# Sums of gathered rows and the next gathers behind a pair's fill while the first places are found

## The chip, the cores and the metric

The kernel runs on one core of a Trainium2 chip. A core has five engines, each with its own in-order queue of instructions: PE (matrix multiplication; results go to PSUM, a small memory of banks), DVE (vector work), ACT (activation functions and copies), POOL (here: places of rows, and the gathers), and SP (which issues DMA transfers). The profile lists PE's loading of weights as PEld. The metric is the device time of one execution in microseconds, as the median of several runs. The profile is of one further execution.

## What is computed

A layer norm of x (2048 tokens, 512 features) feeds two branches, and both are added to x. Branch A is attention with 32 heads of 16 features and one shared key and value. Branch B is a layer of 4096 small experts ("PEER"): for each token and each of 32 heads, scores against two sets of 64 keys give the best two of each, the best two of their four sums name two experts, and each expert adds a gated row.

```python
q1 = q[..., :dk]; q2 = q[..., dk:]
s1 = einsum("nhd,ed->nhe", q1, k1); s2 = einsum("nhd,ed->nhe", q2, k2)
i1 = argsort(-s1)[..., :2]; i2 = argsort(-s2)[..., :2]
cand = t1[..., :, None] + t2[..., None, :]          # four sums per head
top_s, top_e = best two of cand, and their experts
g = softmax(top_s)
act = gelu(einsum("nd,nhkd->nhk", xn, u[top_e]))
out = einsum("nhk,nhk,nhkd->nd", g, act, v[top_e])
return x + attention(xn) + out
```

## The kernel before

The 2048 tokens are 16 tiles of 128, in four blocks (phases) of 4 tiles. Experts are handled in two ways. For tokens of blocks 0 and 1 the rows of u and v are **gathered**: one indirect DMA on POOL (L1231) fetches, for 128 tokens, one expert's row of u and of v each (4 KB a token) into one of 12 buffers (`NGB`). There are 512 such gathers. For blocks 2 and 3 a dense form is used, with one-hot rows and matmuls against all experts.

**Places.** `score_thread` finds which experts each token takes. Its order `SEQ` is block 0 with chunks 0 to 7 (a chunk is four heads), block 1 with chunks 0 and 1, block 2 with 0 to 7, then the dense work of block 2, block 1 with 2 to 7, and block 3. While it does block 0 it also makes the weights of the next chunk (`wp_make`: matmuls pw L648, transposes pwt L661, ACT's scaled copy L663, squaring passes L619, and DVE's low half L664). One `item` is 12 matmuls psc (L720), 8 MAX8 (L733) and 4 FIND_INDEX8 (L740) on DVE. After four items `batch` makes the indices on POOL (L784 to L809) and puts four entries into the dictionary `IDX`. psc, pw and pwt share three PSUM tiles (tag x).

**The paired loop.** From the loop `for d in range(half + 24)` on, each step d handles a pair of key blocks of attention, by `att_steps`. The instructions are issued in the order in which the code runs, and each engine takes its own in that order:

1. two score tiles (PE sc L452, two PSUM tiles of tag s, and ACT's exponential L459),
2. the value products of the step before (PE pv L469),
3. `mid()`: on ACT the tanh of finished gathers (L1259), squaring passes over expert rows (L1379) and other waiting items; on DVE the dot products of gathered u rows (`dots`, L1243) and the weights of the sums (`weigh`, L1266, which needs the tanh); then the closure `go`,
4. two more score tiles and exponentials,
5. `fill()`: `run_scores` takes pieces of `score_thread` until a sum of assumed costs is reached, and then runs what stands in `POST_FILL`.

**The closure `go`** has four kinds of work: the sums of gathered v rows into the token's accumulator (`adds`, DVE L1278, two or three a step); the items of `CHAIN`, three small DVE instructions after every fourth dot (gq L1252, gy L1253, ga L1254; gy is the input of the tanh of the next step); the items of `rest`, such as the gates of a batch (L792, L814 to L816); and up to four new gathers, each into the buffer that a sum has just read. Now and then it also queues the store of a finished token tile. `go` runs at once inside `mid`, so ahead of items 4 and 5, but for the time in which one-hot rows are formed (`dense_on[0] == 2`): then it stands in `POST_FILL`, behind the fill.

A copy on POOL that the first step issues starts at 121.5 us (L1445). `IDX` is only added to: four entries for each batch of blocks 0 and 1, and none for blocks 2 and 3. `NC` is 8 and `TPH` is 4.

Of the kernel before, what the change touches and what calls it, by code (L numbers as in the profile page):

```python
# [33 lines left out]
NC = 8  # L34
TPH = GT
# [26 lines left out]
def tile_kernel(ctx, tc, exact, flag, x, wq, wkv, wo, wqT, kT, uv, ub, vb, out):  # L62
# [519 lines left out]
    def experts_out(t):  # L582
        acc, last = ACC[t], t // GT == QB[3]
        assert last or t in DONE_A
        store(lambda: nc.sync.dma_start(d_part[t] if last else out[t * P:(t + 1) * P, :], acc))
        LIVE.discard(t)
# [102 lines left out]
    def met_most():  # L689
        assert meets[0] == NPH * NC  # L690
        m = PK["met"] = small.tile([P, 1], F32, name="mm", bufs=1)
        nc.vector.reduce_max(m, most.rearrange("p t h k -> p (t h k)"), axis=AX.X)

    def met_flag():
        m = PK.pop("met")
        p = xtile("pm")
        nc.tensor.transpose(p[:1, :P], m, ident)
        r = small.tile([1, 1], F32, name="prd", bufs=1)
        nc.vector.reduce_max(r, p[:1, :P], axis=AX.X)
        nc.vector.tensor_scalar(flag, r, 0.0, None, op0=OP.is_ge)  # L700
# [44 lines left out]
    IDX, G = {}, {}  # L745
# [516 lines left out]
    def weigh(n):  # L1262
        if n not in WT and n < a_ready[0] // SB:
            ga, th = GA.pop(n), TH.pop(n)
            w = small.tile([P, SB], F32, name="w", bufs=3)
            nc.vector.scalar_tensor_tensor(w, th, 1.0, ga, op0=OP.add, op1=OP.mult)  # L1266
            WT[n] = w
# [17 lines left out]
    def gathers(most):  # L1285
        while g_next[0] < NSL and g_next[0] < a_next[0] + NGB - lent[0] and most > 0:
            gather(g_next[0])
            g_next[0] += 1
            most -= 1

    def dots(to):
        while d_next[0] < min(to, NSL):
            dot(d_next[0])
            d_next[0] += 1

    def adds(most):
        while a_next[0] < a_ready[0] and most > 0:
            add(a_next[0])
            a_next[0] += 1
            most -= 1  # L1300

    def tanhs(to):
        while a_ready[0] + SB <= to:
            tanh(a_ready[0] // SB)
            a_ready[0] += SB
# [8 lines left out]
    def run(fns):  # L1314
        todo = fns[:]
        fns.clear()
        for fn in todo:
            fn()
# [6 lines left out]
    def flush():  # L1325
        posts()
        for _ in range(2):
            for fns in (ON_ACT, PARTS, LAST, LATER, BEHIND):
                run(fns)
            ON_ACT.extend(LATER_ACT)  # L1330
            LATER_ACT.clear()
        run(ON_ACT)
        run(BEHIND)
# [65 lines left out]
    def norm_steps(d):  # L1399
        j, r = divmod(d - 24, 2)  # L1400
        if r == 0 and 0 <= j < NB // 2:
            NU[j] = norm_rows(j)
        j, r = divmod(d - 26, 2)
        if 0 <= j < NB // 2:
            on_act(lambda t=NU[j]: norm_sum(j, t, r))
        if d == 58:
            norm_most()
        if d == 60:
            norm_factors()

    dense_on, quiet = [0], [0]
# [3 lines left out]
    def run_scores(until=None, key=None):  # L1415
        while (until is not None and spent[0] < until) or (key is not None and key not in IDX):
            posts()
            try:
                cost = next(sgen)
            except StopIteration:  # L1420
                spent[0] = 1e9
                posts()
                return
            if cost is None:

                if key is None:
                    return
                continue
            spent[0] += cost

    STEPS = 512


    def att_steps(d, mid, fill):
        i = 2 * d
        run(STORES)
# [16 lines left out]
        if 0 < i <= STEPS:  # L1453
# [3 lines left out]
            if pk == 14:  # L1457
                unit_tail(pu)
        mid()
        if 0 < i < STEPS:  # L1460
            scores(u, kc + 1, 0)
# [40 lines left out]
    def score_steps(n):  # L1502
        for _ in range(n):
            spent[0] += next(sgen)
# [122 lines left out]
    with tc.manual_schedule(engines=ENGINES):  # L1627
        nc.vector.tensor_copy(PK["mm"][96:128], PK["mm"][:32])
        run(AFTER)
        score_steps(3)  # L1630
        done0 = spent[0] - 5.4
        half = STEPS // 2
        pos, since = 0.0, half
        for d in range(half + 24):


            if dense_on[0] != 0:
                since = d
            if dense_on[0] == 1:
                pos += 2.35 if d < half * 3 // 4 else max(0.0, NSL - pos) / max(half - 3 - d, 1)  # L1640
            else:
                pos += (2.6 if len(IDX) < NC * TPH else 2.45 if 0 <= d - since < 32 else 2.05, 0, 0.25, 1.5, 0.5)[dense_on[0]]

            todo = max(min(int(pos + 0.001), g_next[0]) - d_next[0], 0) if d else 0

            def mid():
                post = POST[:]
                POST.clear()
                for act, _ in post:
                    act()  # L1650
                tanhs(d_next[0])
                room = ROOM - 0.65 * len(ON_ACT) - 0.7 * len(LAST)
                run(ON_ACT)
                ON_ACT.extend(LATER_ACT)
                LATER_ACT.clear()
                run(LAST)
                while PARTS and (room > 0.7 or len(PARTS) > 3):
                    PARTS.pop(0)()
                    room -= 0.75
                LAST.extend(LATER)  # L1660
                LATER.clear()
                rest = BEHIND[:]
                BEHIND.clear()

                dots(d_next[0] + todo - 1)
                if a_ready[0] > a_next[0]:
                    weigh(a_next[0] // SB)
                dots(d_next[0] + 1 if todo > 0 else 0)
                for _, fn in post:
                    fn()  # L1670
                sums = min(a_ready[0] - a_next[0], max(todo, 3) if d < half else 4)
                if dense_on[0] > 2:
                    sums = min(sums, 2)
                if quiet[0] > 0:
                    quiet[0] -= 1
                    sums = 0
                if dense_on[0] == 2:
                    run(CHAIN)

                def go():  # L1680
                    n = sums
                    while rest or CHAIN or n > 0:
                        if n > 0:
                            adds(1)
                            n -= 1
                        elif not rest:
                            run(CHAIN)
                        if CHAIN:
                            CHAIN.pop(0)()
                        if rest:  # L1690
                            rest.pop(0)()
                    gathers(4)

                    for _ in range(1 if d < half - 4 else NT):
                        if OUTS:
                            experts_out(OUTS.pop(0))

                if dense_on[0] == 2:
                    POST_FILL.append(go)
                else:  # L1700
                    go()

            aim = done0 + (FILL - done0) * (d + 1) / half if d < half else 1e6

            def fill():
                run_scores(until=min(aim, spent[0] + MOST))
                run(POST_FILL)

            norm_steps(d)
            att_steps(d, mid, fill)  # L1710
            if d == half - 26 and not exact:
                met_most()
            if d == half - 16 and not exact:
                met_flag()
        flush()
        run(STORES)
        while a_next[0] < NSL:
            dots(NSL)
            run(CHAIN)
            tanhs(d_next[0])  # L1720
            adds(SB)
            run(STORES)
            gathers(NGB)
        assert not OUTS
        run(STORES)
# [42 lines left out]
```

## Time and profile before

| | |
|---|---|
| median of 3 runs | 1788.83 us (1785.12 to 1790.47) |
| the profiled execution | 1779.54 us, its span 1777.7 us |
| granted PE clock, mean | 0.991 |
| DMA, mean of the span | 265 GB/s |
| gathers (L1231) | 512, 1068 ns of POOL each |
| sums (L1278) | 512, 744 ns of DVE each |
| dots (L1243) | 512, 681 ns of DVE each |

How to read the rows. A row of the groups has line, engine, operation, tiles written and read, shapes and count, then busy us, mean ns of one, and the idle time of the engine just before them with what ended it. A row of the timeline has start, duration, engine, line, operation; in brackets stands the idle time before it and its releaser. A row of the waits has who waited for whom, us in total, times, and the longest. In the table of stretches each engine has its busy us and its count, then come the granted clock of PE (1.00 is full), the share of the DMA engines and GB/s. "issue" is idle time for which the profile shows no cause.

### The profile page before, as it was taken

The page shows a single profiled execution, that of the slowest core. Times are in us where ns is not written, and L with a number is a line of the kernel's source. Part 1 is how long each engine was busy: PE and PEld are TensorE (multiplying, and loading weights), DVE is VectorE, ACT ScalarE, POOL GpSimd, SP SyncE. Part 2 cuts the span into 40 slices and gives each one's busy share as a digit, 9 for nine tenths or more (in the row PEclk, how much of TensorE's full clock was granted, in tenths as well). Part 3 has the DMA queues.
Part 4 walks back from the last instruction along what each step waited for, and adds up shares of the span by engine and source line. Part 5 has one row for each costly group of instructions (what it writes and reads, how often), then busy time and mean ns, then how long its engine had stood idle before and what let it go on. Part 6 is the DMA issues. An engine that isn't in the chain of part 4 may idle for free.

```text
span 1777.7 us, 34221 instructions
## 1 busy us (share of the span) xinstructions
PE 1692.0 (95%) x11071; PEld 598.4 (34%) x11071; DVE 1534.4 (86%) x5385; ACT 1329.0 (75%) x1793; POOL 709.5 (40%) x983
## 2 busy tenths in 40 slices
PE   7989998999999889999999999999998999999997
PEld 3433333333333333333333333333333333333332
DVE  7648888989999977988998898999999778888894
ACT  6468787867777988888988666666679877777773
POOL 1024454555663103433433356566640124444430
PEclk9999999999999999999999999999999999999999
DMA  7378888999983469999899977877653779999892
GB/s 263 128 243 310 278 297 286 307 335 337 330 277 138 159 214 296 301 309 320 290 350 318 334 271 250 281 265 255 195 183 111 257 235 291 305 324 313 262 313 70
DMA packets 257277, 471.02 MB, mean 265 GB/s; under 512 B 107316, under 2 KB 118596, under 8 KB 257084
## 3 DMA queue, kind: packets, MB, share of 16 engines
q0 software_dynamic: 73728, 268.47, 43.7%
q1 hardware_dynamic: 182940, 199.59, 34.8%
q8 instruction: 89, 1.46, 0.3%
q14 instruction: 104, 0.85, 0.1%
q10 hardware_dynamic: 416, 0.66, 0.1%
HBM read 407.36 MB, written 56.39 MB: 261 GB/s over the span
## 4 chain that ended last, share of the span: by engine, by line
PE 67%; DVE 15%; ACT 6%; issue 2%; DMA 2%; ACTq 0%; SPq 0%; DVEq 0%
PE pv L469 20%; PE psc L720 13%; PE sc L452 12%; PE pout L1109 9%; PE pact L967 8%; ACT pt L459 4%; DVE xa L1278 2%; PE pwo L569 2%; DVE oh L1025 2%; DVE g L1243 2%; DVE i L740 2%; DVE m L733 2%; PE pw L648 1%; DVE obs L1028 1%; DVE obs L1027 1%
## 5 line engine op out<-in xcount | busy, mean ns | idle before, releaser
L459 ACT ACTIVATE pt<-sc 128x1024 f32<-128x1024 f32 x1024 | 990.2, 1026 | 318.6 <-PE sc L452 317.5
L1231 POOL DMA_INDIRECT g<-in_uv_dram,idx x512 | 546.6, 1068 | 866.6 <-DVE xa L1278 429.9
L469 PE MATMUL pv<-pt,vaug 128*32 128x512 f32 x4096 | 497.8, 604 | 0.0
L1278 DVE SCALAR_TENSOR_TENSOR xa<-g,w,xa 128x512 f32<-128x512 f32 x512 | 372.4, 744 | 0.1
L720 PE MATMUL psc<-wk,xt 128*128 128x512 f16 x1536 | 357.7, 381 | 5.1 <-DVE wk L664 5.1
L452 PE MATMUL sc<-qa,kaug 64*128 64x512 f16 x2048 | 323.5, 383 | 37.7 <-ACT pt L459 33.7
L1243 DVE CUSTOM_DVE_ANT_0 g<-g,xa 128x512 f32<-128x512 f32 x512 | 333.8, 681 | 0.0
L720 PEld LDWEIGHTS <-xt 128*128 128x128 f16 x1536 | 141.2, 98 | 202.7 <-issue 54.1
L452 PEld LDWEIGHTS <-kaug 64*128 64x128 f16 x2048 | 82.1, 94 | 375.3 <-issue 369.3
L469 PEld LDWEIGHTS pv<-pt,vaug 128*32 128x32 f32 x4096 | 107.6, 110 | 255.9 <-issue 255.9
L967 PE MATMUL pact<-xt,wk 128*128 128x512 f16 x768 | 181.5, 381 | 0.0
L1109 PE MATMUL pout<-wk,wd 128*128 128x512 f16 x768 | 175.8, 379 | 0.0
L733 DVE MAX8 m<-psc 128x8 f32<-128x64 f32 x1024 | 145.7, 212 | 18.3 <-PE psc L720 18.2
L740 DVE FIND_INDEX8 i<-m,psc 128x8 uint32<-128x128 f32 x512 | 138.4, 285 | 0.0
L1109 PEld LDWEIGHTS <-wd 128*128 128x128 f16 x768 | 73.0, 98 | 92.5 <-issue 7.9
L967 PEld LDWEIGHTS <-wk 128*128 128x128 f16 x768 | 68.9, 98 | 99.5 <-issue 26.3
L1025 DVE TENSOR_TENSOR oh<-io,tr 128x2048 f16<-128x2048 f16 x64 | 77.8, 1216 | 5.1 <-PE pg L1063 4.8
L1182 DVE SCALAR_TENSOR_TENSOR gy<-gy,pact 128x512 f32<-128x512 f32 x60 | 41.0, 683 | 36.3 <-ACT gy L1181 35.6
L1266 DVE SCALAR_TENSOR_TENSOR w<-gth,ga 128x4 f32<-128x4 f32 x128 | 20.5, 160 | 55.8 <-ACT gth L1259 55.6
L1112 DVE SCALAR_TENSOR_TENSOR da<-pout,cols,da 128x512 f32<-128x512 f32 x72 | 53.4, 745 | 14.5 <-PE pout L1109 14.4
L784 POOL CAST fi<-i 128x32 f32<-128x32 uint32 x60 | 12.6, 240 | 106.3 <-DVE i L740 106.3
L918 DVE SCALAR_TENSOR_TENSOR wk<-rw,cols,wk 128x512 f16<-128x512 f32 x64 | 47.3, 743 | 6.5 <-ACT wk L911 6.5
(238 smaller groups left out, 1499.9 us busy)
## 6 DMA issues: line engine op xcount, KB each, us to landing
wk<-dw SPq DMA_DIRECT2D x96, 256.0 KB
wqt<-in_wqT_dram SPq DMA_DIRECT2D x32, 512.0 KB
un<-in_uv_dram SPq DMA_DIRECT2D x16, 1024.0 KB
ds<-wk SPq DMA_DIRECT2D x64, 256.0 KB
gates<-dg SPq DMA_DIRECT2D x64, 256.0 KB
wk<-ds SPq DMA_DIRECT2D x64, 256.0 KB
dg<-gst SPq DMA_DIRECT2D x14, 928.0 KB
dw<-wk SPq DMA_DIRECT2D x32, 256.0 KB
```

The source lines that it names most:

```text
L452: nc.tensor.matmul(p[:, b, :], kaug[o:o + 64, kc * P:(kc + 1) * P], QA[u][o:o + 64, i, :], start=True, stop=True)
L459: nc.scalar.activation(PT[u, kc, i], p, AF.Exp, scale=SCALE)
L469: nc.tensor.matmul(PV[u][32 * j:32 * j + 32, :], vaug[:, kc, :], pt[:, b, :], start=kc == 0, stop=kc == 15)
L720: nc.tensor.matmul(p, XT[kk][:, a, j * P:(j + 1) * P], WC[n_][kk][:, bb, :], start=n == 0, stop=n == 11)
L733: nc.vector.max(m8[:, jb, s // 2, SECOND * (s % 2):][:, :8], p[:, s * E:(s + 1) * E])
L740: nc.vector.max_index(i8[:, jb, h, :8], m8[:, jb, h, :8], p[:, h * P:(h + 1) * P])
L967: nc.tensor.matmul(p, us[:, a, k * P:(k + 1) * P], XT[k][:, c, :], start=n == 0, stop=n == 11)
L1025: nc.vector.tensor_tensor(out=oa, in0=num(P), in1=bc(0, tb, P), op=OP.is_equal)
L1109: nc.tensor.matmul(p, wd[0][:, a, j * P:(j + 1) * P], vs[:, c, :], start=n == 0, stop=n == last)
L1231: nc.gpsimd.indirect_dma_start(out=gt, out_offset=None, in_=uv, in_offset=bass.IndirectOffsetOnAxis(ap=IDX[ph, c, ti][:, s:s + 1], axis=0))
L1243: nc.vector.tensor_tensor_reduce(u, u, XN[TPH * ph + ti], scale=1.0, scalar=0.0, op0=OP.mult, op1=OP.add, accum_out=a[:, i:i + 1])
L1278: nc.vector.scalar_tensor_tensor(acc, v, w[:, i:i + 1], acc, op0=OP.mult, op1=OP.add)
```

## The change

One condition is widened: `go` is also put behind the fill while `IDX` has fewer than NC * TPH = 32 entries. The same expression already sets the pace of the dots in the loop, a few lines earlier.

```diff
-                if dense_on[0] == 2:
+                if dense_on[0] == 2 or len(IDX) < NC * TPH:
                     POST_FILL.append(go)
                 else:
                     go()
```

In the steps concerned, `go`'s DVE work is then issued behind the MAX8, FIND_INDEX8 and low-half instructions of the step's fill, and its gathers behind the POOL work of a batch that ends in that fill. What PE, ACT and SP are given, and in which order, stays as it is.

## The prediction

> **What bounds the kernel now.** I read the page first: span, engine shares and the chain that ended last.
>
> ```profile
> span 1777.7 us, 34221 instructions
> PE 1692.0 (95%) x11071; PEld 598.4 (34%) x11071; DVE 1534.4 (86%) x5385; ACT 1329.0 (75%) x1793; POOL 709.5 (40%) x983
> PE 67%; DVE 15%; ACT 6%; issue 2%; DMA 2%; ACTq 0%; SPq 0%; DVEq 0%
> ```
>
> PE is busy 95% of the span and carries two thirds of the chain. The order of every engine is written out by hand and the change alters no matmul, so the time can only change where PE stands still. First I need the stretch in which the new condition holds. It counts entries of `IDX`: four per batch of places, and NC * TPH is 8 * 4 = 32. So it ends with the eighth batch, the last of token block 0. The rows of `idx`, and the eighth of them on POOL's timeline:
>
> ```profile
> L809 POOL CAST idx<-fi x16: 211/228/676, 88.2 to 1157.5; 128x32 int32<-128x32 f32 x16
> 359.95 0.21 POOL L809 CAST idx<-fi 128x32 int32<-128x32 f32 x1
> ```
>
> The paired loop starts about 121 us, and its first step that sees 32 entries is the one that begins near 356 us. Blocks 1 and 2 add two batches of `IDX` and none, and come later. So the stretch is 121 to about 360 us, not that of three blocks. The table by stretches (busy us per engine, then the granted clock, DMA share, GB/s), the third a part of the first:
>
> ```profile
> 121.00:362.00 241.00, 227.48 (x1404) 79.43 (x1403) 206.44 (x916) 192.87 (x281) 119.91 (x170) 0.98 0.87 293
> 362.00:545.00 183.00, 180.12 (x1106) 60.72 (x1105) 173.50 (x926) 136.14 (x188) 109.15 (x207) 0.99 0.89 309
> 195.00:198.50 3.50, 3.50 (x17) 0.80 (x18) 3.36 (x20) 1.48 (x3) 2.02 (x7) 0.51 0.97 346
> ```
>
> PE is idle 241 - 227.5 = 13.5 us there, and at a clock of 0.98 it loses another 0.02 * 241 = 4.8 us. These 18 us, 1.0% of the span, are all that the change can win at most. The view of waits of this stretch says who ends PE's idle time (us in total, times, longest):
>
> ```profile
> DVE wk L664 <- ACT wk L663: 13.1, 12, 3.0
> DVE m L733 <- PE psc L720: 9.1, 6, 2.8
> ...
> DVE w L1266 <- ACT gth L1259: 8.2, 8, 2.4
> ...
> PE psc L720 <- DVE wk L664: 5.1, 5, 2.0
> ...
> PE sc L452 <- ACT pt L459: 3.5, 5, 1.2
> ...
> PE pw L648 <- issue: 2.4, 1, 2.4
> PE pwt L661 <- DVE i L740: 2.4, 1, 2.4
> ```
>
> The four PE rows make 13.4 us. The largest waits for the low half of a new weight tile on DVE (L664), which frees one of three PSUM tiles of tag x. But that instruction was itself held by ACT's copy (L663), 13.1 us in 12 waits. The second is ACT's exponential. The last two, 4.8 us, wait for a MAX8 and FIND_INDEX8 series, as the rows of one show:
>
> ```profile
> 296.49 1.46 PE L720 MATMUL psc<-wk,xt 128*128 128x512 f16 x6
> ...
> 298.00 1.14 DVE L733 MAX8 m<-psc 128x8 f32<-128x64 f32 x8
> ...
> 300.30 1.48 PE L648 MATMUL pw<-wqt,kTs 128*64 128x512 f32 x4 [2.36 <-issue]
> ```
>
> The psc matmuls before this MAX8 end at 296.49 + 1.46 = 297.95, so MAX8 was not late. **No PE stall of the stretch is one that the sums of gathered rows made.**
>
> **The change part by part.** The moved closure holds a step's sums (L1278), the small chain that prepares the next tanh (L1252 to L1254), the gate instructions of a batch (7 times), and up to four gathers on POOL. It adds and removes no instruction. Nothing of it goes to SP: the stores of finished tiles come only with the last chunk, later than this. One step of before, DVE and ACT from the timeline:
>
> ```profile
> 213.62 0.67 DVE L1243 CUSTOM_DVE_ANT_0 g<-g,xa 128x512 f32<-128x512 f32 x1
> ...
> 215.74 0.75 DVE L1278 SCALAR_TENSOR_TENSOR xa<-g,w,xa 128x512 f32<-128x512 f32 x1
> 217.14 0.15 DVE L1253 SCALAR_TENSOR_TENSOR gy<-gq,act 128x4 f32<-128x4 f32 x1
> ...
> 217.98 0.75 DVE L664 SCALAR_TENSOR_TENSOR wk<-pwt,cols,wk 128x512 f16<-128x512 f32 x1
> 218.65 1.14 DVE L733 MAX8 m<-psc 128x8 f32<-128x64 f32 x8
> ...
> 220.77 0.67 DVE L1243 CUSTOM_DVE_ANT_0 g<-g,xa 128x512 f32<-128x512 f32 x1
> ```
>
> DVE runs dots, then sums and chain (215.74 to 217.98, 2.2 us), then the fill's work. In the new order the 2.2 us stand between 220.77 and the next dots. Three things follow.
>
> (a) **The tanh.** Its input gy is ready 1.55 us after the first sum (217.29 - 215.74). Now it is ready 1.55 us after the fill's last DVE instruction. The tanh waits at a fixed place on ACT, behind the next pair's first two exponentials and ahead of its last two and of all copies of the fill:
>
> ```profile
> 220.77 0.21 ACT L1259 ACTIVATE gth<-gy 128x4 f32<-128x4 f32 x1
> 221.34 1.03 ACT L459 ACTIVATE pt<-sc 128x1024 f32<-128x1024 f32 x1 [0.36 <-PE sc L452]
> ...
> 227.42 3.77 ACT L459 ACTIVATE pt<-sc 128x1024 f32<-128x1024 f32 x4
> ...
> 228.50 0.39 PE L452 MATMUL sc<-qa,kaug 64*128 64x512 f16 x2 [1.05 <-ACT pt L459]
> ```
>
> Here gy would come at 220.77 + 1.55 = 222.3, so ACT stands idle 1.5 us and the exponential of 221.34 starts 1.2 us later. ACT then runs squaring passes and copies without a pause and does not recover: the exponentials at 227.42 come about 1.2 us later, and PE's stall of 1.05 us grows by as much. How often? The groups of the stretch:
>
> ```profile
> L1259 ACT ACTIVATE gth<-gy 128x4 f32<-128x4 f32 x21 | 4.4, 210 | 0.0
> ...
> L459 ACT ACTIVATE pt<-sc 128x1024 f32<-128x1024 f32 x132 | 127.8, 1024 | 28.7 <-PE sc L452 28.4
> ...
> L619 ACT ACTIVATE junk<-wqt 128x1024 bf16<-128x1024 f32 x22 | 23.3, 1065 | 0.0
> L1379 ACT ACTIVATE un<-un 128x1024 f32<-128x1024 f32 x8 | 8.5, 1057 | 0.0
> ```
>
> There are 132 / 4 = 33 steps and 21 tanhs. None waits for its input now. Set against the end of the fill of the step before, as above, some five would still not wait and the others would wait 0.5 to 3 us, about 20 us in all. ACT's idle time is 241 - 192.9 = 48 us, 1.5 us a step, so most is absorbed; but 30 passes of 1.06 us (22 + 8) lie unevenly, and where one or more stand in the step ACT has no room. Bounds: 0 (all absorbed) and 20 us (all reaches PE). I take five tanhs at 1.1 us, 5.5 us, nearer to the first end because the mean idle time of a step is as long as a typical delay.
>
> (b) **The gathers.** A gather needs its buffer's sum, so it is issued with the sums, some 5 to 7 us later than now, while its dot comes only 2.2 us later. The tightest, with its dot, and the landing times of the stretch (min, median, max):
>
> ```profile
> 287.72 1.28 POOL L1231 DMA_INDIRECT g<-in_uv_dram,idx  x1 [11.44 <-DVE gq L1252]
> ...
> 293.31 0.68 DVE L1243 CUSTOM_DVE_ANT_0 g<-g,xa 128x512 f32<-128x512 f32 x1
> ...
> 294.53 0.69 DVE L1243 CUSTOM_DVE_ANT_0 g<-g,xa 128x512 f32<-128x512 f32 x1
> ```
>
> ```profile
> DMA to landing us min/median/max: 4.3/6.2/9.2
> ```
>
> Now its step's sums would start after the fill, at the 293.31 of the next step's first dot, and the gather at about 294.3; it lands 4.3 us later at best, 298.6, while the dot would be due at 294.53 + 2.2 = 296.7. DVE waits 1.9 us, the MAX8 of 298.00 moves by about 1.4, and so does the end of PE's stall at 300.30. In seven steps POOL's own batch work (L784 to L809) now also stands ahead of the gathers. Other gathers have over 2.5 us to spare before the dot; I take this one and little else: 1.5 us. Bounds 0 and 6 us (four such).
>
> (c) **Earlier MAX8 and low halves.** They no longer stand behind the sums. What PE waited for was held by ACT or by PE's own matmuls (above), so I take -0.5 us; bounds 0 and -4 us, as part of the 4.8 us behind FIND_INDEX8. DVE has 241 - 206.4 = 35 us of idle time for the sums in their new place, 1 us a step; what is late next is the next step's dots, covered by PE's three x tiles.
>
> (d) **The clock.** The row 195.00:198.50 above is at 0.51. It follows a stall of PE:
>
> ```profile
> 194.43 2.15 PE L720 MATMUL psc<-wk,xt 128*128 128x512 f16 x6 [1.96 <-DVE wk L664]
> ```
>
> Such a stretch costs 0.49 * 3.5 = 1.7 us. I take 0.3 of one more such stretch, 0.5 us; bounds -5 (all three of this stretch gone) and +5 (three more).
>
> The Trainium skill, TensorE: Matmul & The Clock Gate, section What's actually happening, has the clock halved after at least one idle window of about 3.4 us. By it no stall of 1 to 2.4 us would cost any clock, and the sum would be 6.5; the trace shows halved stretches right behind such stalls, so it doesn't agree, and I keep the 0.5.
>
> Sum: 5.5 + 1.5 - 0.5 + 0.5 = **+7 us**. The profiled execution took 1779.54 us (span 1777.7), 9.3 us less than the median of the runs, 1788.83. I put the 7 us on both: 1786.5 for such an execution, 1795.8 for the median. After 360 us nothing is moved, and PE, busy 98% and more in the next stretch, has no room to give the loss back.
>
> **The rivals.** *All absorbed*: ACT's 48 us of idle time takes the tanh delays and no gather is late. The mean of 1.5 us a step speaks for it, the back-to-back rows around 226 us against it. Time: 1788.8 +- 3.
>
> *A gain*: dots and MAX8 close up, x tiles come free earlier, ACT is fed earlier, and PE's stalls and their halved clock shrink by half of 18 us: 1788.8 - 9 = 1780. It decides if the low halves or MAX8 really ended PE's waits on DVE's account; the rows 13.1 and 9.1 us speak against it.
>
> *A cascade*: late gathers hold DVE, DVE holds gy, gy holds ACT. Each loop adds, and PE's new stalls bring the halved clock: 12 us of stalls and two stretches of 1.7 us, 1788.8 + 15 = 1804. It decides when the delays pass 1.5 us in most steps.
>
> *The change covers what it says*: with all three blocks it would run to 545 us. DVE is idle only 9.5 us there; I'd add 5 us, 1801. The count of `IDX` speaks against it.
>
> **How the numbers follow.** A measurement of this kernel can tell about 0.3%, 5.4 us, from no change: below 1783.5 is faster, above 1794.2 slower. Forecast (+3 to +12): 0.55, of it 0.37 above 1794.2 and 0.18 below. Absorbed: 0.16, all same. Gain: 0.13, of it 0.12 faster. Cascade: 0.14, and three blocks 0.02, slower. So faster 0.12, same 0.35, slower 0.53. The range 1784 to 1807 leaves out about 0.1 at each end. The forecast's own range is 1792 to 1801.
>
> **What would show it.** Right: in 121 to 362 us ACT's tanh group has idle time ended by DVE gy, 10 to 25 us, where it has 0.0 now; PE's idle time grows from 13.5 to about 20 us, most of it in waits for ACT pt and DVE wk; past the stretch the timeline is the old one, shifted. (b) is seen as DVE dots that wait for DMA, at all. Wrong: PE's idle time falls, or the shift arises after 362 us.

## The result, and the profile after

| | before | after |
|---|---|---|
| median of 6 runs | 1788.24 us | 1812.86 us (1808.96 to 1815.5) |
| the profiled execution | 1779.54 us | 1812.23 us, its span 1810.5 us |
| ratio after to before | | 1.0151, 95% interval 1.0132 to 1.0169 |

One of the six executions of before took 2418.94 us; the ratio is that of fast runs, and the other five of before lie between 1781.10 and 1790.47 us. The change makes the kernel 1.5% slower, some 27 us by the ratio (the two medians lie 24.6 us apart). The forecast was +7 us, 1795.8, with a range up to 1807. The direction was right, the size was not.

The page of after: the span, the busy shares, the chain that ended last, and three groups of instructions.

```profile
span 1810.5 us, 34228 instructions
...
PE 1697.3 (94%) x11071; PEld 599.3 (33%) x11071; DVE 1537.7 (85%) x5385; ACT 1327.4 (73%) x1793; POOL 713.9 (39%) x983
...
PE 62%; DVE 17%; ACT 7%; issue 4%; DMA 2%; another core or an unknown queue 1%; ACTq 0%; SPq 0%; DVEq 0%
...
L452 PE MATMUL sc<-qa,kaug 64*128 64x512 f16 x2048 | 327.2, 384 | 62.1 <-ACT pt L459 54.2
...
L1243 DVE CUSTOM_DVE_ANT_0 g<-g,xa 128x512 f32<-128x512 f32 x512 | 335.1, 683 | 19.3 <-DMA g<-in_uv_dram,idx 16.9
...
L784 POOL CAST fi<-i 128x32 f32<-128x32 uint32 x60 | 12.4, 235 | 127.8 <-DVE i L740 127.4
```

The work is the same, the waits are not. The same three groups of before:

```profile
L452 PE MATMUL sc<-qa,kaug 64*128 64x512 f16 x2048 | 323.5, 383 | 37.7 <-ACT pt L459 33.7
L1243 DVE CUSTOM_DVE_ANT_0 g<-g,xa 128x512 f32<-128x512 f32 x512 | 333.8, 681 | 0.0
...
L784 POOL CAST fi<-i 128x32 f32<-128x32 uint32 x60 | 12.6, 240 | 106.3 <-DVE i L740 106.3
```

Three numbers stand out. Over the whole span the score matmuls wait 20 us more for ACT's exponentials. The dots never waited for a gather, and now do for 16.9 us. POOL's index work (L784) waits 21 us more for the FIND_INDEX8 ahead of it.

**Where the time arises.** The table of stretches: busy us per engine, then the granted clock, the DMA share, GB/s. First before, then after, cut so that both first rows hold the same work: past it, the exponentials of after come about 25 us later than those of before.

```profile
121.00:375.00 254.00, 240.48 (x1484) 83.84 (x1483) 219.33 (x973) 202.98 (x294) 126.30 (x176) 0.98 0.87 297
```

```profile
121.00:400.00 279.00, 243.53 (x1465) 83.19 (x1462) 218.71 (x970) 199.85 (x292) 130.78 (x175) 0.96 0.81 277
...
400.00:571.00 171.00, 169.90 (x1048) 57.87 (x1045) 163.54 (x873) 128.34 (x177) 104.44 (x203) 1.00 0.84 293
```

The stretch takes 279 us where it took 254. PE's idle time grows from 254 - 240.5 = 13.5 to 279 - 243.5 = 35.5 us, and its busy time by 3.05 us at the lower clock: 22 + 3 = 25 us. In the stretch behind it PE is idle for 1.1 us in 171, so nothing is lost there and nothing comes back. (The two profiled executions lie 32.7 us apart. 9.3 us of that was the lead of the profiled before over its median; the later shift from 25 to 34 us comes in a few single steps. The largest, 5 us at about 928 us, is not in a second profile of after; that one has other, smaller ones, so how much of the later shift belongs to the change stays open.)

**Who waits.** The waits of after in 121 to 400 us (who for whom; us in total, times, longest):

```profile
POOL fi L784 <- DVE i L740: 31.3, 7, 6.0
...
DVE wk L664 <- ACT wk L663: 17.9, 13, 2.3
...
PE sc L452 <- ACT pt L459: 17.2, 19, 3.4
DVE g L1243 <- DMA g<-in_uv_dram,idx: 16.9, 8, 4.9
...
ACT gth L1259 <- DVE gy L1253: 13.1, 9, 2.9
...
ACT gth L1259 <- DVE gg L815: 10.2, 3, 5.5
...
PE psc L720 <- DVE wk L664: 7.1, 5, 2.0
...
PE pw L648 <- issue: 4.7, 1, 4.7
```

Of PE's 22 us of new stalls 17.2 - 3.5 = 13.7 (3.5 being the row of before in the prediction) lie ahead of score matmuls that wait for ACT. One of these waits, 3.39 us at 395.52, stands behind an exponential that itself waited 5.07 us for "remote", which stands for another core or an unknown queue; the second profile of after has such a wait of 4.37 us too, and before has none. What it was is not known. ACT's tanh waits for gy: the profile puts some of these waits down to other instructions of DVE (gg, xa, or "issue"), but the tanh reads only gy, and each of its 16 waits in this stretch, 28.5 us in all, ends within 0.05 us of the end of a gy. DVE waits for a gather, POOL for FIND_INDEX8. A POOL row that waits costs nothing by itself; what counts is what stands behind it. In before, around the last batch but one, three gathers stand ahead of the index work (POOL's timeline from the third of them on: start, duration, line, releaser):

```profile
332.65 0.94 POOL L1231 DMA_INDIRECT g<-in_uv_dram,idx  x1 [0.30 <-DVE m L733]
334.08 0.37 POOL L784 CAST fi<-i 128x32 f32<-128x32 uint32 x2 [0.49 <-DVE i L740]
...
339.18 0.21 POOL L809 CAST idx<-fi 128x32 int32<-128x32 f32 x1
339.91 1.02 POOL L1231 DMA_INDIRECT g<-in_uv_dram,idx  x1 [0.52 <-DVE m L733]
```

In after the same batch runs from 348.93 to 354.87 us, and these gathers stand behind it. The timeline of after, all engines:

```profile
354.66 0.21 POOL L809 CAST idx<-fi 128x32 int32<-128x32 f32 x1
...
355.39 1.02 POOL L1231 DMA_INDIRECT g<-in_uv_dram,idx  x1 [0.52 <-DVE m L733]
...
359.18 3.74 ACT L459 ACTIVATE pt<-sc 128x1024 f32<-128x1024 f32 x4
...
360.24 0.39 PE L452 MATMUL sc<-qa,kaug 64*128 64x512 f16 x2 [1.23 <-ACT pt L459]
...
361.15 0.39 PE L452 MATMUL sc<-qa,kaug 64*128 64x512 f16 x2 [0.52 <-issue]
361.47 2.82 PE L469 MATMUL pv<-pt,vaug 128*32 128x512 f32 x16
363.45 0.69 DVE L1243 CUSTOM_DVE_ANT_0 g<-g,xa 128x512 f32<-128x512 f32 x1 [4.90 <-DMA g<-in_uv_dram,idx]
...
364.07 1.15 DVE L733 MAX8 m<-psc 128x8 f32<-128x64 f32 x8
...
366.20 0.73 DVE L1278 SCALAR_TENSOR_TENSOR xa<-g,w,xa 128x512 f32<-128x512 f32 x1
...
368.27 0.15 DVE L1253 SCALAR_TENSOR_TENSOR gy<-gq,act 128x4 f32<-128x4 f32 x1
...
368.46 0.20 ACT L1259 ACTIVATE gth<-gy 128x4 f32<-128x4 f32 x1 [5.54 <-DVE gg L815]
...
369.61 3.74 ACT L459 ACTIVATE pt<-sc 128x1024 f32<-128x1024 f32 x4
...
370.67 0.47 PE L452 MATMUL sc<-qa,kaug 64*128 64x512 f16 x2 [1.80 <-DMA xt<-dxt]
```

Read it downwards from the first gather behind the batch, which starts at 355.39 (the PE rows at 360.24 and 361.15 belong to the round before). Its dot waits 4.90 us for it, until 363.45. MAX8 stands behind that dot, the sums behind the fill (366.20), the gates among the sums, and gy comes at 368.27. ACT's tanh has then held the queue for 5.54 us, and the four exponentials of the next pair start behind it and a squaring pass. PE then stands still for 1.80 us, until 370.67. The profile puts this down to a transfer of xt, but PE starts 1.06 us after the exponentials, the same distance as from 359.18 to 360.24, so it may as well have waited for the first of them. This is one whole round from a late gather to PE's input.

### The profile page after: what moved, and what is told of

Same layout as the page of the kernel before. It is cut to its first block, busy times and chain, and to the rows that moved or that the text cites. A ratio compares the mean times of both kernels' runs of the same rounds, so it can differ in the third digit from the quotient of the medians.

```text
span 1810.5 us, 34228 instructions
## 1 busy us (share of the span) xinstructions
PE 1697.3 (94%) x11071; PEld 599.3 (33%) x11071; DVE 1537.7 (85%) x5385; ACT 1327.4 (73%) x1793; POOL 713.9 (39%) x983
## 4 chain that ended last, share of the span: by engine, by line
PE 62%; DVE 17%; ACT 7%; issue 4%; DMA 2%; another core or an unknown queue 1%; ACTq 0%; SPq 0%; DVEq 0%
PE pv L469 19%; PE sc L452 11%; PE psc L720 11%; PE pout L1109 8%; PE pact L967 8%; ACT pt L459 5%; DVE xa L1278 3%; PE pwo L569 2%; DVE m L733 2%; DVE i L740 2%; DVE g L1243 2%; DVE oh L1025 2%; PE pw L648 1%; DMA dinv<-rc 1%; DVE wk L664 1%
## 5 line engine op out<-in xcount | busy, mean ns | idle before, releaser
L452 PE MATMUL sc<-qa,kaug 64*128 64x512 f16 x2048 | 327.2, 384 | 62.1 <-ACT pt L459 54.2
L1243 DVE CUSTOM_DVE_ANT_0 g<-g,xa 128x512 f32<-128x512 f32 x512 | 335.1, 683 | 19.3 <-DMA g<-in_uv_dram,idx 16.9
L733 DVE MAX8 m<-psc 128x8 f32<-128x64 f32 x1024 | 146.3, 215 | 28.2 <-PE psc L720 18.3
L1112 DVE SCALAR_TENSOR_TENSOR da<-pout,cols,da 128x512 f32<-128x512 f32 x72 | 53.5, 747 | 14.1 <-PE pout L1109 11.6
L784 POOL CAST fi<-i 128x32 f32<-128x32 uint32 x60 | 12.4, 235 | 127.8 <-DVE i L740 127.4
L1266 DVE SCALAR_TENSOR_TENSOR w<-gth,ga 128x4 f32<-128x4 f32 x128 | 20.5, 160 | 48.7 <-ACT gth L1259 46.1
```

The costliest lines, as they stand in the source:

```text
L452: nc.tensor.matmul(p[:, b, :], kaug[o:o + 64, kc * P:(kc + 1) * P], QA[u][o:o + 64, i, :], start=True, stop=True)
L733: nc.vector.max(m8[:, jb, s // 2, SECOND * (s % 2):][:, :8], p[:, s * E:(s + 1) * E])
L1243: nc.vector.tensor_tensor_reduce(u, u, XN[TPH * ph + ti], scale=1.0, scalar=0.0, op0=OP.mult, op1=OP.add, accum_out=a[:, i:i + 1])
```

## The experiments

Each kernel was compared with before on the same chip. Three parts of the moved closure can be placed apart: the **chain** (with the gates), the **sums**, and the **gathers**; the fourth thing is where POOL's **batch** of index work stands against the gathers. In the table "late" is behind the fill, "first" is late, but ahead of the sums, and us is (ratio - 1) times the median of before on the same chip (1777.06 us for the first three kernels and for the next stretch, 1783.83 to 1784.78 for the others, 1788.24 for the first after). The last columns are waits in 121 to 400 us of each profile: dots for gathers, the tanh's idle time, and PE's score matmuls for ACT. A faster kernel has more of its work in this window: of the 6.4 us of before, 3.5 lie ahead of 375 us, where it has done what after does by 400.

| kernel | chain | sums | gathers | batch | ratio (95%) | us | dots | tanh | PE |
|---|---|---|---|---|---|---|---|---|---|
| before | early | early | early | behind | | 0 | 0.0 | 0.0 | 6.4 |
| e2 | late | early | early | behind | 1.0006 (0.9982 to 1.0029) | 1.1 | 0.0 | 5.5 | 4.5 |
| e1 | early | late | late | ahead | 1.0096 (1.0068 to 1.0125) | 17.1 | 21.3 | 6.7 | 6.8 |
| e3 | first | late | late | ahead | 1.0065 (1.0039 to 1.0090) | 11.6 | 23.5 | 16.7 | 9.2 |
| after | late | late | late | ahead | 1.0151 (1.0132 to 1.0169) | 27.0 | 16.9 | 28.5 | 17.2 |
| e0, after again | late | late | late | ahead | 1.0161 (1.0134 to 1.0187) | 28.7 | 15.9 | 24.0 | 14.9 |
| e6 | late | late | late | behind | 1.0125 (1.0084 to 1.0167) | 22.3 | 5.0 | 21.5 | 11.9 |
| e7 | first | late | late | behind | 1.0059 (1.0039 to 1.0080) | 10.5 | 6.7 | 10.7 | 11.6 |
| e9 | early | late | late | behind | 1.0057 (1.0038 to 1.0077) | 10.2 | 6.8 | 4.3 | 7.9 |
| e8 | early | early | late | ahead | 1.0158 (1.0131 to 1.0184) | 28.2 | 21.8 | 1.9 | 12.2 |
| e10 | early | early | late | behind | 1.0004 (0.9983 to 1.0026) | 0.7 | 0.0 | 0.0 | 4.3 |

### Only the sums and the gathers late (e1)

```diff
-                if dense_on[0] == 2 or len(IDX) < NC * TPH:
+                if dense_on[0] == 2:
+                    POST_FILL.append(go)
+                elif len(IDX) < NC * TPH:
+                    run(CHAIN)
+                    run(rest)
                     POST_FILL.append(go)
```

> In the stretch of block 0 only the sums and the gathers go behind the fill; the chain (gq, gy, ga) and the gates stay where they were before, in the middle of the step. Tanh theory (the late gy holds ACT, and ACT holds PE): gy is early again, so the loss of 25 us falls to 0 to 8 us, and ACT's tanh has under 3 us of idle time ahead of it in this stretch (28 us with the change). Gather theory (late sums make late gathers, and DVE's dots wait for them): the loss stays at 15 to 25 us, with 15 us or more of DVE waiting for gathered rows (19 us with the change). If each needs the other, about 8 to 15 us.

Measured: +17.1 us (interval 12.1 to 22.2), as the gather theory has it. The dots wait 21.3 us for gathers. The tanh's idle time falls from 28.5 to 6.7 us, in two waits, so most of this loss needs no late tanh.

### Only the chain and the gates late (e2)

```diff
+                def chain_late(items):
+                    run(items)
+                    run(rest)
...
+                elif len(IDX) < NC * TPH:
+                    items = CHAIN[:]
+                    CHAIN.clear()
+                    adds(sums)
+                    gathers(4)
+                    POST_FILL.append(lambda: chain_late(items))
```

> The other half: sums and gathers stay in the middle of the step, only the chain and the gates go behind the fill. Tanh theory: 15 to 25 us slower than before, with 15 us or more of ACT idle ahead of the tanh. Gather theory: 0 to 8 us slower, no DVE wait for gathered rows. If each needs the other, 5 to 15 us.

Measured: no difference (+1.1 us, interval -3.2 to +5.2). The groups of e2 in 121 to 400 us (count, busy us, mean ns, idle time before them and its releaser):

```profile
L452 PE MATMUL sc<-qa,kaug 64*128 64x512 f16 x312 | 49.0, 384 | 4.6 <-ACT pt L459 4.5
...
L1243 DVE CUSTOM_DVE_ANT_0 g<-g,xa 128x512 f32<-128x512 f32 x97 | 62.9, 683 | 0.0
...
L1259 ACT ACTIVATE gth<-gy 128x4 f32<-128x4 f32 x24 | 5.0, 210 | 5.5 <-DVE gy L1253 5.5
```

The tanh waits for gy as foreseen, but only 5.5 us in all, and PE does not wait longer for the exponentials. Behind the fill the chain alone costs nothing that can be measured. Here, however, no sum stands between the fill and gy.

### The chain ahead of the sums (e3)

```diff
                 def go():
                     n = sums
+                    if first:
+                        run(CHAIN)
+                        run(rest)
```

Here `first` is `len(IDX) < NC * TPH`, taken in `mid`; all of `go` stays behind the fill.

> As the changed kernel, but within the closure the chain and the gates come first and the sums after them, so gy is ready some 0.7 to 1.5 us earlier behind the fill, and the gathers 0.3 to 1 us later. Tanh theory: of the 25 us at least 8 are gone (15 to 17 us slower than before or less). Gather theory: no gain, 24 to 28 us slower than before.

Measured: +11.6 us, although the dots wait 23.5 us for gathers, more than in after. What falls is the tanh's idle time, from 28.5 to 16.7 us, and PE's waits for ACT, from 17.2 to 9.2. The gather theory had foreseen no gain.

### The same move in the next stretch alone (e5)

```diff
-                if dense_on[0] == 2 or len(IDX) < NC * TPH:
+                if dense_on[0] == 2 or NC * TPH <= len(IDX) <= NC * TPH + 2 * TPH and dense_on[0] == 0 and d < half // 2:
```

> The same move in the next stretch alone (blocks 1 and 2 up to the one-hot rows, about 360 to 545 us), where no weights are made, ACT is busy 74% and DVE 95%. Tanh theory: ACT has idle time enough, 0 to 6 us slower. Gather theory: DVE has 9.5 us of idle time there and cannot take any wait, 8 to 20 us slower.

Measured: 1.0037 (1.0013 to 1.0061), +6.6 us. The move costs something in both stretches, and four times as much in the first; the time lies between the ranges of the two theories. In 362 to 571 us of its profile the dots wait for no gather, although the index work of nine batches falls into it, and the tanh waits 16.2 us for gy (0.0 in before).

### After once more (e0), and dots held back (e4)

The first is after unchanged, the second keeps the dots at least three gathers behind the newest one:

```diff
-            todo = max(min(int(pos + 0.001), g_next[0]) - d_next[0], 0) if d else 0
+            behind_by = 3 if d > 2 and len(IDX) < NC * TPH else 0
+            todo = max(min(int(pos + 0.001), g_next[0] - behind_by) - d_next[0], 0) if d else 0
```

> The changed kernel once more, on the chip of the next three runs, as their yardstick and for a second profile: 1.3 to 1.7% slower than before. If the 5 us by which its first profile fell back at 928 us belong to the change, they are there again; if they are chance, they are not.

> As the changed kernel, but while places of block 0 are found the dots stay at least 3 gathers behind the newest gather, so each gather has about one step more to land. Gather theory: DVE's waits for gathered rows fall from 17 to under 5 us, and the loss from 27 us to 5 to 14. Tanh theory: the loss stays above 20 us, since the chain is still behind the fill.

Measured: +28.7 us for after, and 1.0124 (1.0103 to 1.0146), +22.1 us, with the dots held back. The dots still wait 16.5 us for gathers (15.9 without the edit), so it did not do what it was made for, and says nothing on the price of that wait.

### POOL's batch behind the gathers (e6), and with the chain first too (e7)

In e6 all index work of a batch of block 0 but the first (L784 to L809) is put into `POST_FILL`, behind `go`; e7 adds the edit of e3.

```diff
-            G_.tensor_scalar(i1, i1, float(E), None, op0=OP.mult)
...
-            G_.tensor_copy(idx, i1)
+            def places():
+                G_.tensor_scalar(i1, i1, float(E), None, op0=OP.mult)
...
+                G_.tensor_copy(idx, i1)
+
+            if later:
+                POST_FILL.append(lambda: (split_places(), places()))
+            else:
+                places()
```

> As the changed kernel, but in the stretch the POOL instructions of a batch (L784 to L809 of before) are issued behind the step's gathers and not ahead of them. Gather theory in its narrow form (it is the batch ahead of the gathers that makes them late, 7 times 4 to 5 us): DVE's waits for gathered rows fall to under 6 us and the loss to 4 to 12 us. Gather theory in its wide form (the sums' later place alone makes them late): the waits stay at 10 us or more and the loss at 18 us or more. Tanh theory: no change, 24 to 28 us. A FIND_INDEX8 of the next chunk now waits for casts that stand behind gathers; if that costs, it shows as DVE waiting for POOL.

> The last one with the chain and the gates ahead of the sums in the closure. If late gathers and a late gy add, it is the best of the moved forms: 0 to 6 us slower than before. If the gathers alone count, as the last one within 3 us. If the sums' place alone counts, 12 us or more slower.

Measured: +22.3 us (interval 15.0 to 29.8) and +10.5 us. The groups of e6, then of e7, in 121 to 400 us (lines behind L784 have moved by 13, so L1256 are the dots, L1266 gy, L1272 the tanh):

```profile
L1256 DVE CUSTOM_DVE_ANT_0 g<-g,xa 128x512 f32<-128x512 f32 x93 | 60.5, 685 | 5.0 <-DMA g<-in_uv_dram,idx 5.0
...
L1272 ACT ACTIVATE gth<-gy 128x4 f32<-128x4 f32 x22 | 4.5, 206 | 21.5 <-DVE gy L1266 18.6 <-DVE gq L1265 1.3 <-DVE gg L828 0.9
```

```profile
L1256 DVE CUSTOM_DVE_ANT_0 g<-g,xa 128x512 f32<-128x512 f32 x95 | 62.1, 685 | 6.7 <-DMA g<-in_uv_dram,idx 6.7
...
L1272 ACT ACTIVATE gth<-gy 128x4 f32<-128x4 f32 x23 | 4.9, 212 | 10.7 <-DVE gy L1266 10.3 <-issue 0.4
```

The batch was what made most gathers late: without it ahead of them the dots' waits fall from 16 to 5 us, as foreseen. The time hardly follows (28.7 to 22.3 us, with intervals that overlap, where 4 to 12 were foreseen); the tanh still waits 21.5 us. With the chain ahead of the sums as well, that halves, and so does the loss, though not to the 0 to 6 us that were expected.

### Only the gathers late, with the batch ahead and behind (e8, e10), and e1 with the batch behind (e9)

```diff
-                    gathers(4)
+                    if len(IDX) < NC * TPH:
+                        POST_FILL.append(lambda: gathers(4))
+                    else:
+                        gathers(4)
```

with the condition of `go` as in before. e10 is this with the batch as in e6, e9 is e1 with the batch as in e6.

> Only the new gathers are issued behind the fill in the first stretch; sums, gates and chain stand where they stood before, inside mid. Theory A (what the sums-late kernel lost, 17 us, it lost through late gathers): the gathers are as late as there, and the dots do not move back, so the DVE dots wait 15 to 25 us in all for DMA (19.5 in the sums-late kernel), and the time is 10 to 20 us above before. Theory B (the loss comes from the sums' place on DVE, between a fill's low half and the next dots): with the sums back in place the time is within 4 us of before, whatever the dots wait. Under both, ACT's tanh of gathered rows waits more than in before (0.0) only as far as DVE waited for DMA.

> As the sums-late kernel (chain and gates early, sums and gathers behind the fill), and POOL's batch of places is issued behind the step's gathers. Theory A (late gathers): the dots' waits for DMA fall from 19.5 to below 7 us, PE's waits for the low half from 11.7 to about 5, and the time to 0 to 6 us above before. Theory B (the sums' place on DVE): the waits for DMA fall likewise, but the time stays 10 to 17 us above before.

> As the gathers-late kernel (only the gathers behind the fill; sums, gates and chain in their old place, which cost 28 us), and POOL's batch of places is issued behind the step's gathers, so that a gather waits for nothing on POOL but the order of its own queue. Theory A (the price of late gathers is the wait of POOL's batch for the fill's last FIND_INDEX8, with the gathers queued behind it): the dots' waits for DMA fall from 21.8 to below 7 us and the time to 0 to 8 us above before. Theory B (a gather that is issued behind the fill's POOL work at all is too late, with or without the batch): waits of 12 us and more stay, and the time stays 15 us and more above before.

Measured: +28.2 us for e8, +0.7 for e10, +10.2 for e9. e8 is beyond the 10 to 20 us of theory A, e9 lies at the lower end of theory B, e10 is as theory A has it. Gathers that alone are moved behind the fill cost as much as the whole change. The timeline of e8 shows one batch:

```profile
159.18 0.44 POOL L784 CAST fi<-i 128x32 f32<-128x32 uint32 x2 [11.14 <-DVE i L740]
...
164.06 0.21 POOL L809 CAST idx<-fi 128x32 int32<-128x32 f32 x1
...
164.42 1.03 POOL L1231 DMA_INDIRECT g<-in_uv_dram,idx  x1 [0.15 <-issue]
...
168.75 0.69 DVE L1243 CUSTOM_DVE_ANT_0 g<-g,xa 128x512 f32<-128x512 f32 x1 [2.48 <-DMA g<-in_uv_dram,idx]
```

POOL stands still for 11.14 us, with the gathers in its queue, until the fill's last FIND_INDEX8 is done; then the index work takes 164.27 - 159.18 = 5.1 us; only then do the gathers go, and the dots wait. In e10 the gathers are issued behind the fill as well, but ahead of the batch. That gives POOL and DVE practically the order of before, so it is a control as much as a repair. The groups of e8, then of e10:

```profile
L1243 DVE CUSTOM_DVE_ANT_0 g<-g,xa 128x512 f32<-128x512 f32 x91 | 59.9, 687 | 22.9 <-DMA g<-in_uv_dram,idx 21.8 <-issue 1.1
...
L784 POOL CAST fi<-i 128x32 f32<-128x32 uint32 x14 | 2.6, 217 | 70.2 <-DVE i L740 70.2
```

```profile
L1256 DVE CUSTOM_DVE_ANT_0 g<-g,xa 128x512 f32<-128x512 f32 x97 | 62.9, 684 | 0.0
...
L787 POOL CAST fi<-i 128x32 f32<-128x32 uint32 x18 | 3.5, 225 | 10.0 <-DVE i L740 10.0
```

In e10 POOL waits 10.0 us for FIND_INDEX8 with no gather of the step behind it, and nothing is lost; in e8 it waits 70.2 us ahead of the gathers, and they wait with it. In e9 POOL's index work waits 0.1 us for FIND_INDEX8, and 10 us remain: with the sums behind the fill a gather still can't go before its sum, and the dots wait 6.8 us.

### What the runs add up to

Two routes lead from the moved closure to PE. **By POOL:** batch, gather, dot, then MAX8, the low half and gy behind that dot. With nothing else moved it costs 28.2 us (e8), and 0.7 with the batch behind (e10). **By ACT:** fill, sums, gy, tanh, exponential. With the batch behind the gathers the change still costs 22.3 us (e6), of which 12 go when the chain stands ahead of the sums (e7), to the 10 that the late sums cost with the chain early too (e9).

In the changed kernel the second route is the larger part. The chain's place behind the sums is worth 11.8 us with the batch behind (e6 to e7) and 15 to 17 with the batch ahead (after and e0 to e3); both lie outside the intervals. The batch's place is worth 6.4 us (e0 to e6), 6.9 (e1 to e9) or 1.1 (e3 to e7), and each time the intervals overlap. So that the batch costs time is shown only where the sums stay early. The routes don't add: 28 and 22 alone give 27 to 29 together. That both delay the same steps would explain it, and no run shows it.

Open remain three things. Late gathers with early sums cost 28.2 us (e8), with late sums 17.1 (e1), on two chips; that the late sums move the fill's MAX8 forward and the dots back, and so give the gathers time, fits that, but no run shows it. The 10 us of late sums were not split further between the dots' waits and the sums' place on DVE. And in e8 the last step to PE is not seen whole: the tanh waits only 1.9 us there, so gy is not the way, PE waits 12.2 us for exponentials and 9.2 for low halves (5.1 in before), and four exponentials wait 11.8 us in all for "remote". No version was found that beats before: e2 and e10 equal it.

## Why the prediction missed

**The place was right.** The time arises between 121 and 400 us (the old 375), and the table of stretches behind it shows PE idle for 1 us in 171. The direction was right too, and by the mechanism that the forecast named: a late gy. What failed is the size of two terms of the sum, (a) and (b).

**(a) The tanh.** The foreseen wait was about 20 us in all, 10 to 25 in 121 to 362 us. The group of after there:

```profile
L1259 ACT ACTIVATE gth<-gy 128x4 f32<-128x4 f32 x19 | 3.9, 206 | 23.0 <-DVE gy L1253 13.1 <-DVE gg L815 4.7 <-issue 3.4
```

All 23.0 us of it are waits for gy (above). So the wait was sized well. The step that failed is the part of it that reaches PE: 5.5 us were taken, on the ground that the mean idle time of ACT in a step is as long as a typical delay. The chain's place behind the sums costs 22.3 - 10.5 = 12 us (e6, e7), or 15 to 17 with the batch ahead (e3). The text had noted that the passes and copies of ACT lie unevenly, so that a mean of idle time can't be set against the delays step by step; that it priced this too low is the likely reason, and no run varies it. In e2, where the chain stands behind the fill but ahead of any sum, the wait is 5.5 us and costs nothing.

**(b) The gathers.** This term was 1.5 us, with a bound of 6. Sums and gathers behind the fill cost 10 us even with the chain early or first and no batch ahead of them (e9, e7). The text let the gather land 4.3 us after its start, the least time of the stretch, where the median was 6.2; the dot at 363.45 comes 8.06 us after its gather was issued and still had to wait. And it saw that "in seven steps POOL's own batch work (L784 to L809) now also stands ahead of the gathers", and gave it no price. The batch takes 4.6 to 6.2 us of POOL in after, and starts only when the fill's last FIND_INDEX8 is done. In after four of the seven batches hold the dots, 14.7 of the 16.9 us; the other 2.3 us belong to a gather that stands behind no batch. With sums and chain in their old place the batch ahead of the gathers costs 28.2 us (e8); in the change itself 1 to 7, within the noise of the comparisons.

**(c) Earlier MAX8 and low halves** were put at -0.5 us. No gain is seen: PE's waits for the low half went from 5.1 to 7.1 us, and its wait ahead of pw L648 from 2.4 to 4.7. **(d) The clock**, put at 0.5 us with a bound of 5, took 3 us (the busy time above). Its premise, that lowered clocks stand right behind stalls of 1 to 2.4 us, holds for some such stalls only (last section).

**The rivals.** The cascade, which had 0.14, comes nearest with its 15 us: a late gather holds DVE, DVE holds gy, gy holds ACT, as the rows from 355.39 on show. But it is not the whole: e6 takes its first link away, and 22.3 of 28.7 us stay. Nor did it need delays in most steps, as its condition had it: 8 waits of the dots and 16 of the tanh, eight of them above 1.5 us, in about 34 steps. The three blocks did not come into it; the guess of 5 us for the further ones compares with 6.6 measured for the next stretch (e5). The range ended at 1807, 3 us above the cascade's time, so it had no room for (a) at 12 us and (b) at 10 together.

## What to carry to other kernels

When work is moved on an in-order queue, price what it is moved behind: not only the time of that work, but the wait at its head. A wait that costs nothing at the end of a queue (POOL's for FIND_INDEX8, e10) can cost 28 us once transfers with little slack are queued behind it (e8). And where a moved block feeds two engines, order it inside by who waits soonest; here the small chain ahead of the sums took back 12 of 22 us.

## What was not expected of the hardware

PE's clock is lowered behind some short stalls, and not behind others. The 1.23 us that PE stood at 360.24 in the timeline of after, with 0.52 us more right behind, are followed by this row of its table of stretches, in which PE is busy throughout:

```profile
361.20:364.20 3.00, 3.00 (x18) 0.53 (x17) 0.74 (x3) 1.72 (x2) 0.58 (x1) 0.69 1.06 398
```

The 16 value products take 2.82 us there, at a granted clock of 0.69; at 353.20 the same 16 took 1.92 us. In the 3.5 us behind other stalls of after the clock was 0.59 (2.00 us, at 197.87) and 0.50 (4.68 us, at 312.65), but 1.00 behind 1.89 us (160.69), 2.68 us (233.58) and 2.04 us (270.36). So below 3 us the length of a stall does not decide it, and what does is not shown here. The prediction set such stretches against the Trainium skill's page TensorE: Matmul & The Clock Gate, section What's actually happening, where one idle window of about 3.4 us comes first; the lowered clocks behind 1.23 and 2.00 us don't agree with that either.
